# Relative-bias attention and squared-ReLU layers on one core: the turning of one batch's x by DMA, one ring of four PSUM banks, and a new order of the instructions

## The chip, the cores and the metric

The kernel runs on one core of a Trainium2 chip (trn2). The metric is the device time of one execution in microseconds; three runs of the kernel before are given, and the median counts. The profile comes from another execution of the same program, and its own span is the time against which sums are made. A core has five engines with a queue of instructions each: PE (TensorE, matmuls; its loads of the stationary operand are listed as PEld), DVE (VectorE), ACT (ScalarE), POOL (GpSimd) and SP (SyncE, which here only issues DMAs). Each engine works through its own queue in order and waits at an instruction until the semaphores that it names have come.

## The reference

Inputs are `q`, `k`, `v` of shape (8 batches, 8 heads, 576 positions, 64), a table of 32 buckets of bias by head, and two weight matrices, 512 x 2048 and 2048 x 512. What is computed, cut to its core:

```python
scores = scale * q @ k.T + bias_table[bucket(pos_i - pos_j)]
attn = exp(scores - max) / sum(exp(scores - max))
x = (attn @ v) -> 4608 tokens x 512
h = maximum(x @ w_in, 0)
out = (h * h) @ w_out
```

Beyond a distance of 128 all positions share one bucket, so the bias differs from a constant only in a band around the diagonal.

## The kernel before

**Tiles and stages.** A pair is two heads of one batch; there are 32 pairs, four to a batch. For a pair, q and k come from memory as 16-bit numbers into a stage buffer (`stg`, ring of 5), are turned so that the head's 64 numbers lie on partitions (`qt`, `kt`, ring of 4), and the scores are computed with keys on partitions: `run` (L698 to L725) makes four score matmuls of 512 columns (L707) into two PSUM sets (`st`, two banks each, ring of 2), and ACT takes the exponential from there into `pt` (L720). As 576 is 4.5 times 128, the last 64 queries and keys of a pair are done apart: corners of `qt` and `kt` are copied into the buffer `qz` (L689, on DVE or POOL), `last_queries` (L733) and `last_keys` (L758) make their scores, L743 and L768 their exponentials. DVE multiplies the band of `pt` with the table of exponentials of the bias (L801). P.V follows (L837, L844) in two parts of 3 and 2 tiles of 128 queries, each part in one PSUM bank, a column of ones giving the sums; DVE takes reciprocals (L861) and normalises into `x` (L866).

**Turning x.** The layers need x with its features on partitions (`xt`, a ring of three batches). `x_turn` (L894) does it on PE: four transposes of 128 x 128 for each of five tiles (L904), and an eviction by ACT or DVE (L624, L626). It serves the batches under `DT_X` (2). The batches from `DT_X` on are turned by two DMA transposes a pair, issued on SP (L879 to L892). Likewise q and k of batches 0 and 1 are turned on PE (L662), and those of later batches by DMA from SP (L645).

**Layers.** The 4608 tokens are nine groups of 512. In layer 1 (L1257) a group has 16 tiles of four matmuls of 512 columns; ACT applies the relu (L1286), DVE squares (L1296). Layer 2 (`second`, L991) uses Strassen's scheme with seven products instead of eight: sums of the weights (L958) and of the activations (L983) on DVE, then products of 16 matmuls of 256 columns (L1028), collected by fused adds on DVE (L1056) or copies on ACT (L1062). In the last two groups part of layer 1 is done by sevens too (`by_sevens`, L1116): a unit replaces 4 of the 16 tiles by seven products of four matmuls of 256 columns (L1182), with the sums of L1108 and the collecting operations L1207, L1212, L1221, L1230 and L1232. `UNITS` gives the number of units, one for group 7 and two for group 8.

**PSUM.** Eight banks: four for the score sets, one for P.V (`pv_ps`, ring of 1), three for everything else (`g_ps`: table, transposes, layers 1 and 2, ring of 3).

**What sets the order.** Every operation is first put into a plan with its engine or engines, its supposed duration, its dependences, its buffers, a due time and an earliest time (`Plan.add`, L105). `Plan.schedule` (L113) then walks through a model of the engines: at each step it takes, of the operations that can start first, the one that is due first, and gives it a buffer of its ring. The instructions are issued in that order, so the plan's durations and due times decide the order in every queue, and what a wait is placed behind. `LAT` holds supposed delays between engines, `SWITCH` the price of a change between kinds of matmul on PE (modes "c", transposes of 96 rows; "r", scores; "f", all else). `load` puts a DMA's issue on POOL or SP and its transfer on a modelled DMA engine.

**Loads.** POOL issues the loads that cast (q, k, weights, v of batches 0 and 1; L280); v of later batches comes as 32-bit numbers by SP and is cast by POOL (L556). Small fills (L398, with the constants `QUIET` and `LATER` as earliest times) prepare buffers; `s_fix` (L415) are the ten fills of the stages.

```python
def xt_free(upto):
    old = upto - 1 - XR
    return [f1_last[old // GT]] if old >= 0 else []
```

`f1_last` holds the operation of layer 1 that was added last for a group, and a write into `xt` waits for it.

Of the kernel before, what the change touches and what calls it, by code (L numbers as in the profile page):

```python
# [33 lines left out]
DT_X = 2  # L34
RELU_DVE = 0
NSTG, NQK, NPT, NV, NX, NGB, NRT, NY, NF = 5, 4, 3, 3, 6, 2, 4, 4, 2
QUIET, LATER = 5000.0, 9000
# [6 lines left out]
UNITS = {7: 1, 8: 2}  # L44
# [7 lines left out]
def _bucket(n):  # L52
    half = NBK // 2
    max_distance = 128
    log_ratio = np.log(np.maximum(n, 1).astype(np.float32) / half) / np.log(
        max_distance / half
    )
    large = half + (log_ratio * (half - 1)).astype(np.int32)
    large = np.minimum(large, NBK - 1)
    return np.where(n < half, n, large).astype(np.int64)  # L60

# [36 lines left out]
SWITCH = 105.0  # L98


class Plan:
# [11 lines left out]
    def schedule(self):  # L113
# [12 lines left out]
        while len(done) < len(self.ops):  # L126
            best = None
            for e in engines:
                pick = None
                for op in waiting[e]:  # L130
                    at = max(now[e], op.ready, self._buf_time(op))
                    if at == float("inf"):
                        continue
                    key = (max(at, now[e]), op.due if op.due > -1e8 else op.ready - 1e9, op.seq)
                    if pick is None or key < pick[0]:
                        pick = (key, op)
                if pick is None:
                    continue
                if best is None or pick[0][0] < best[0][0]:
                    best = (pick[0], e, pick[1])  # L140
            assert best is not None, "the plan is stuck"
            (at, _, _), e, op = best
            took = op.engs[e]
            if e == "PE" and op.mode != mode:
                took += SWITCH
                mode = op.mode
            for x in op.engs:
                waiting[x].remove(op)
            op.eng, op.start, op.end = e, at, at + took
            now[e] = op.end  # L150
            for b in op.bufs:
                if b.slot is None:
                    t, b.slot = min(b.ring.free)
                    b.ring.free.remove((t, b.slot))
                    b.ring.taken += 1
                b.left -= 1
                b.until = max(b.until, op.end + LAT[e])
                if not b.left:
                    b.ring.free.append((b.until, b.slot))
            for u in op.users:  # L160
                u.wait -= 1
                if not u.wait:
                    u.ready = max(
                        [u.after]
                        + [d.end + (LAT[d.eng] if tuple(u.engs) != (d.eng,) else 0.0) for d in u.deps]
                    )
                    for x in u.engs:
                        waiting[x].append(u)
            done.append(op)
# [15 lines left out]
def mm(n):  # L185
    return n / 2.4 + 2.5
# [11 lines left out]
def kernel(  # L198
# [64 lines left out]
    pv_ps = [psum.tile([128, 512], FP32, name=f"pv{i}") for i in range(1)]  # L263
    g_ps = [psum.tile([128, 512], FP32, name=f"f{i}") for i in range(3)]

    P = Plan()
    r_set, r_pv, r_g, r_lane = Ring(2), Ring(1), Ring(3), Ring(8)
# [7 lines left out]
    def loader(eng_name, eng, out_, in_, packets, deps=(), bufs=(), due=0.0, after=0.0, turn=-1e9):  # L275
# [3 lines left out]
            {eng_name: 720.0 if eng_name == "POOL" else 600.0},  # L279
# [77 lines left out]
    for c in range(6):  # L357
# [11 lines left out]
        o = P.add({"PE": 16 * 55.0}, t_mm, [o_eb, l_oh], [t_b], LEAD + TAB, 0.0, "f")  # L369
# [27 lines left out]
    def fill(ap, value, ns, due, after, deps=()):  # L397
        return P.add({"DVE": ns}, lambda: io(nc.vector.memset(ap, value)), deps, (), due, after)  # L398

    zz = z_sb.bitcast(FP32)  # L400
# [15 lines left out]
        fill(stg[i][w][96:128, 512:640].bitcast(FP32), 0.0, 90.0, 40 + i, 25000.0)  # L416
# [25 lines left out]
    def load_six(p, w):  # L442
# [8 lines left out]
                192 * 75, (), [b_stg[p]], pdue(),  # L451
# [3 lines left out]
    def load_rows(p, w):  # L455
# [8 lines left out]
                512 * 34.5, s_fix, [b_stg[p]], pdue(),  # L464
            )
            for e in range(2)
# [5 lines left out]
                128 * 34.5, s_fix, [b_stg[p]], pdue(),  # L472
# [14 lines left out]
    def load_v_head(b, h):  # L487
# [4 lines left out]
            512 * 34.5, v_fix[min(b, 1)], [b_v[b]], pdue(),  # L492
# [3 lines left out]
    def load_v_tail(b):  # L496
        for e in range(2):
# [4 lines left out]
                256 * 34.5, v_fix[min(b, 1)], [b_v[b]], pdue(),  # L502
# [4 lines left out]
    def load_v(b):  # L507
        for tt in range(4):
# [4 lines left out]
                1024 * 34.5, v_fix[min(b, 1)], [b_v[b]], pdue(),  # L513
# [7 lines left out]
    def load_v_fp32(b):  # L521
# [9 lines left out]
        for tt in range(5):  # L531
            fb = Buf(r_f)
            if tt < 4:
# [5 lines left out]
                        1024 * 19, 760.0,  # L539
                    )  # L540
                ]
            else:
# [5 lines left out]
                        256 * 19, 420.0,  # L548
# [15 lines left out]
    def load_w_in(u):  # L564
# [5 lines left out]
                512 * 102, (), (), pdue(),  # L570
# [3 lines left out]
    def load_w_out(u):  # L574
# [4 lines left out]
            512 * 102, (), (), pdue(),  # L579
# [54 lines left out]
    def pair(p):  # L634
# [5 lines left out]
        for w, dst in ((0, qts), (1, kts)):  # L640
            if b >= DT_QK:
# [9 lines left out]
                evac.append(P.add({"DMA": 1160.0}, None, [o], [qb, b_stg[p]], -1e9))  # L651
# [19 lines left out]
            o = P.add({"PE": 12 * 36.0 if b < SIX else 5 * mm(128)}, tr, l_qk[p, w] + [l_id], [bank, b_stg[p]], T - 3000, after, "c" if b < SIX else "f")  # L671
# [11 lines left out]
        for w, src, dst in ((0, qts, qzs), (1, kts, kzs)):  # L683
            for e in range(2):
# [6 lines left out]
                spread.append(one_of({"DVE": 200.0, "POOL": 320.0} if b < DT_QK else {"POOL": 320.0}, sp, [evac[w]] + z_fix[min(p, 1)], [qb], T - 1000))  # L691
# [135 lines left out]
        for part, qt0, nq in ((0, 0, 3), (1, 3, 2)):  # L827
# [49 lines left out]
            if b >= DT_X:  # L877
# [10 lines left out]
                t = x_last[hp, part] = P.add({"DMA": 232.0 * nq}, None, [t], [xb], -1e9)  # L888
# [35 lines left out]
    def xt_free(upto):  # L924

        old = upto - 1 - XR
        return [f1_last[old // GT]] if old >= 0 else []
# [188 lines left out]
    def by_sevens(g, units, due):  # L1116
# [22 lines left out]
        for u in range(units):  # L1139
# [30 lines left out]
            for n, i in enumerate((1, 6, 2, 5, 7, 3, 4)):  # L1170
# [17 lines left out]
                o = f1_last[g] = P.add(  # L1188
# [3 lines left out]
                )  # L1192
                to, plus, where = reads[i]
# [44 lines left out]
    def layers(g):  # L1238
# [35 lines left out]
        for i in range(16):  # L1274
            if i >= skip and g < NG:
# [5 lines left out]
                f1_last[g] = o  # L1281
# [44 lines left out]

    for op in P.schedule():
# [32 lines left out]
```

The softmax here doesn't subtract the row's maximum and nothing guards it: scores larger than these inputs give would overflow.

## Time and profile before

| what | value |
|---|---|
| runs | 371.63 us (median), 371.18 to 372.67 |
| profiled execution, first to last instruction | 369.4 us |
| instructions | 10030 |
| DMA packets, bytes | 162293, 44.26 MB |
| DMA issues on POOL, of q and of k | 55.4 us x79 and 55.3 us x79 |
| x turned on PE (L904) | 40 matmuls, 3.4 us |
| x turned by DMA (L882) | 48 issues, 1.19 us each (median) |
| layer 1 (L1257), layer 2 (L1028, largest group) | 127.8 us x656, 36.1 us x288 |
| by sevens, collecting adds (L1207) | 15 of 0.69 us |

The page gives the span of the profiled execution and not the time around it; the median of the runs is 2.2 us above that span. Where the page or an answer names a line, that is the line of the kernel before. "A <- B" among the waits means that the engine of A stood idle until B was done; times there are the total, the count and the longest. Durations of matmuls overlap their neighbours, so two starts are a better price than one duration. The row "DMA to landing" of a tile counts from the start of the issue to the semaphore that tells of the transfer's end.

### The profile page before, as it was taken

The numbers are of one execution on the slowest core, as the hardware profiler recorded it, in microseconds if no ns is written. First come the engines' busy times: TensorE is split into PE (matmuls) and PEld (weight loads), VectorE is DVE, ScalarE is ACT, GpSimd is POOL, SyncE is SP. The second block draws the span as 40 slices with busy tenths as digits, with TensorE's granted clock in tenths as the row PEclk, the third lists the DMA queues.
The fourth block names the chain that finished last, engine by engine and source line by source line (L and its number), as shares of the span: only waits on it lengthen the run. The fifth ranks groups of instructions, "written<-read, shape, count | busy, mean of one in ns | idle before, by whom it ended". The sixth has DMA issues, their size and how long they took to land.

```text
span 369.4 us, 10030 instructions
## 1 busy us (share of the span) xinstructions
PE 353.9 (96%) x3966; PEld 246.0 (67%) x3966; DVE 277.0 (75%) x618; ACT 262.5 (71%) x377; POOL 185.4 (50%) x343
## 2 busy tenths in 40 slices
PE   3978999899999999999999999999999999999996
PEld 2656455556587457877785468745876689657885
DVE  3997789957785498658965687669755987888693
ACT  4998989688575887689766887688758880586420
POOL 8897359295655676757845556777614100000000
PEclk9999999999999999999999999999999999999999
DMA  9999999795999999998999999999985112200022
GB/s 171 156 135 172 187 175 93 96 112 94 175 113 146 165 128 140 132 167 150 125 130 149 114 161 108 157 169 141 108 124 130 46 36 63 88 2 28 30 86 87
DMA packets 162293, 44.26 MB, mean 120 GB/s; under 512 B 145734, under 2 KB 162246, under 8 KB 162246
## 3 DMA queue, kind: packets, MB, share of 16 engines
q0 software_dynamic: 74208, 14.53, 52.0%
q1 hardware_dynamic: 87696, 28.80, 42.2%
q8 instruction: 31, 0.51, 0.6%
q10 hardware_dynamic: 342, 0.30, 0.3%
q14 instruction: 16, 0.13, 0.1%
HBM read 36.88 MB, written 9.44 MB: 125 GB/s over the span
## 4 chain that ended last, share of the span: by engine, by line
PE 88%; DVE 7%; ACT 2%; DMA 1%; issue 1%; ACTq 0%; DVEq 0%
PE f L1257 32%; PE f L1028 29%; PE pv L844 9%; PE st L707 8%; PE pv L837 2%; DVE pt L801 2%; PE st L758 2%; PE st L733 2%; PE st L1182 1%; DVE x L866 1%; DMA g<-in_q_dram 1%; PE f L662 1%; PE f L363 1%; ACT pm L768 1%; PE pv L1182 1%; DVE s L983 1%
## 5 line engine op out<-in xcount | busy, mean ns | idle before, releaser
L720 ACT ACTIVATE pt<-st 128x1024 f16<-128x1024 f32 x128 | 127.4, 1026 | 30.8 <-PE st L707 30.8
L1257 PE MATMUL f<-xt,w_in_sb 128*128 128x512 f16 (+4 forms) x656 | 127.8, 338 | 0.2 <-ACT xt L624 0.2
L1286 ACT ACTIVATE rt<-f 128x512 f16<-128x512 f32 x132 | 77.8, 602 | 38.4 <-PE f L1257 35.3
L1257 PEld LDWEIGHTS <-w_in_sb 128*128 128x128 f16 x656 | 57.9, 98 | 52.1 <-issue 12.2
L1296 DVE TENSOR_TENSOR g<-rt 128x512 f16<-128x512 f16 x132 | 57.6, 441 | 20.8 <-ACT rt L1286 19.8
L801 DVE TENSOR_TENSOR pt<-pt,tb_sb 128x1536 f16<-128x1536 f16 (+2 forms) x96 | 60.7, 640 | 15.6 <-ACT pt L720 15.1
L1028 PEld LDWEIGHTS <-g 128*128 128x128 f16 x576 | 54.5, 98 | 13.0 <-issue 4.7
L280 POOL DMA_DIRECT2D qs<-in_q_dram x79 | 55.4, 716 | 4.4 <-DMA w_out_sb<-in_moe_w_out_dram 2.6
L280 POOL DMA_DIRECT2D ks<-in_k_dram x79 | 55.3, 702 | 0.7 <-issue 0.6
L844 PE MATMUL pv<-va,pt 128*128 128x65 f16 x1280 | 54.7, 193 | 0.0
L844 PEld LDWEIGHTS <-pt 128*128 128x128 f16 x1280 | 50.2, 97 | 3.2 <-issue 1.4
L1056 DVE SCALAR_TENSOR_TENSOR y<-f,y 128x512 f32<-128x512 f32 (+1 forms) x47 | 31.4, 667 | 23.8 <-PE f L1028 23.6
L1028 PEld LDWEIGHTS <-s 128*128 128x128 f16 x432 | 41.2, 98 | 9.0 <-issue 2.5
L707 PE MATMUL st<-qt,kt 64*128 64x512 f16 x256 | 40.3, 385 | 0.9 <-ACT pt L743 0.4
L689 POOL COPY qz<-kt 64x64 f16<-64x64 f16 x58 | 18.5, 319 | 44.4 <-DMA kt<-ks 34.7
L689 POOL COPY qz<-qt 64x64 f16<-64x64 f16 x61 | 18.9, 310 | 35.4 <-DMA qt<-qs 27.3
L837 PE MATMUL pv<-vm,pm 128*128 128x130 f16 x160 | 35.3, 221 | 1.2 <-DVE x L866 1.0
L1028 PE MATMUL f<-w_out_sb,s 128*128 128x256 f16 x288 | 36.1, 273 | 0.0
L1028 PE MATMUL f<-wt,g 128*128 128x256 f16 x288 | 35.7, 273 | 0.0
L1028 PE MATMUL f<-w_out_sb,g 128*128 128x256 f16 x272 | 34.5, 273 | 0.7 <-ACT y L1062 0.7
L866 DVE TENSOR_TENSOR x<-pv,r 128x384 f16<-128x384 f32 x64 | 31.4, 490 | 2.0
L983 DVE TENSOR_TENSOR s<-g,s 128x1024 f16<-128x1024 f16 x36 | 25.6, 711 | 0.4
(90 smaller groups left out, 338.7 us busy)
## 6 DMA issues: line engine op xcount, KB each, us to landing
out_dram<-y SPq DMA_DIRECT2D x34, 256.0 KB, 2.4
f<-in_v_dram SPq DMA_DIRECT2D x24, 256.0 KB, 4.3
qs<-in_q_dram POOLq DMA_DIRECT2D x48, 64.0 KB, 4.4
ks<-in_k_dram POOLq DMA_DIRECT2D x48, 64.0 KB, 3.5
w_in_sb<-in_moe_w_in_dram POOLq DMA_DIRECT2D x4, 512.0 KB, 7.2
w_out_sb<-in_moe_w_out_dram POOLq DMA_DIRECT2D x4, 512.0 KB, 10.6
qs<-in_q_dram POOLq DMA_DIRECT2D x7, 144.0 KB, 4.6
ks<-in_k_dram POOLq DMA_DIRECT2D x7, 144.0 KB, 5.5
```

The lines of the kernel that those rows point to most:

```text
L280: lambda: io(eng.dma_start(out=out_(), in_=in_())),
L689: io(eng.tensor_copy(out=dst[qb.slot][rw, rw], in_=src[qb.slot][rw, 512:576]))
L707: nc.tensor.matmul(sets_ps[st.slot][:, e, :], kt[rw, ts(jt, 128)], qt[rw, 0:512], start=True, stop=True,)
L720: nc.scalar.activation(out=p5(pts[pb.slot])[:, jt, :, 0:512], in_=sets_ps[st.slot], func=EXPF, scale=SCALE)
L801: io(nc.vector.tensor_tensor(out=a, in0=a, in1=t, op=MULT))
L837: nc.tensor.matmul(ps[:, i, :, :], pm[:, c : c + 128], vm[:, hp, :, 0:65], start=True, stop=False)
L844: nc.tensor.matmul(ps[:, i, e, :], pt[:, (2 * jt + e) * S + c : (2 * jt + e) * S + c + 128], va[:, jt, 2 * hp + e, 0:65], start=False, sto ...
L866: nc.vector.tensor_tensor(out=xs[xb.slot][:, qt0 : qt0 + nq, :].rearrange("p t (e d) -> p t e d", e=2), in0=ps[:, :, :, 0:64], in1=rs[rb.s ...
L1028: nc.tensor.matmul(home[bf.slot][:, ts(s_, HALF)], left(c, s_), right(c), start=(c == 0 and (s_ == 0 or apart) and (own or i not in before ...
L1257: nc.tensor.matmul(g_ps[bank.slot][:, a:z], w_in_sb[:, kk, ts(nt, 128)], xt_sb[:, kk, c : c + z - a], start=(kk == 0), stop=(kk == 3),)
L1286: io(nc.scalar.activation(out=rts[rb.slot], in_=g_ps[bank.slot], func=RELUF))
L1296: nc.vector.tensor_tensor(out=gs[gb1.slot][:, nt, :], in0=rts[rb.slot], in1=rts[rb.slot], op=MULT)
```

## The change

1. `DT_X` goes from 2 to 1: x of batch 1 is turned by DMA transposes on SP as that of the later batches. PE loses 20 transposes, ACT and DVE five evictions, SP gets eight transposes.
2. `pv_ps` and `g_ps` become one list of four banks with one ring: P.V takes any of them, as do layers 1 and 2 and the transposes.
3. `UNITS` gives group 7 two units: 12 tiles of layer 1 become 8, and 28 matmuls of 256 columns are added.
4. The plan's durations are altered (issues, packets, transposes, copies), an engine's next operation may start before the one ahead has ended (`OVER`), and dependences within an engine get a delay (`AGAIN`). `QUIET` and `LATER` are 1000, so the fills may come at the start. The ten fills of `s_fix` may go to POOL or DVE.
5. A table `DUES` replaces the due time of 135 operations by number, after the plan is made.
6. `f1_last` becomes a list: a write into `xt` waits for all operations of layer 1 of the older group.

```diff
-DT_X = 2
+DT_X = 1
-QUIET, LATER = 5000.0, 9000
+QUIET, LATER = 1000.0, 1000.0
-UNITS = {7: 1, 8: 2}
+UNITS = {7: 2, 8: 2}
+DUES = """
+24:58480 30:161030 31:56140 56:-23560 57:13220 58:-12190 60:-19700 61:14570 62:-30210 63:122610 64:-31640
...
+"""
+STAY = 0.0
+OVER = {"ACT": 123.0, "DVE": 85.0, "POOL": 40.0}
+AGAIN = {"ACT": 30.0, "DVE": 30.0}
...
-            now[e] = op.end
+            now[e] = op.end - (OVER.get(e, 0.0) if op.fn is not None else 0.0)
...
-    pv_ps = [psum.tile([128, 512], FP32, name=f"pv{i}") for i in range(1)]
-    g_ps = [psum.tile([128, 512], FP32, name=f"f{i}") for i in range(3)]
+    g_ps = pv_ps = [psum.tile([128, 512], FP32, name=f"f{i}") for i in range(4)]
-    r_set, r_pv, r_g, r_lane = Ring(2), Ring(1), Ring(3), Ring(8)
+    r_set, r_g, r_lane = Ring(2), Ring(4), Ring(8)
+    r_pv = r_g
...
+    def fill_late(ap, ns, due, after):
+        def emit(o):
+            io((nc.vector if o.eng == "DVE" else nc.gpsimd).memset(ap, 0.0))
+
+        o = one_of({"DVE": ns, "POOL": ns}, emit, (), (), due)
+        o.after = o.ready = after
+        return o
...
-        fill(stg[i][w][96:128, 512:640].bitcast(FP32), 0.0, 90.0, 40 + i, 25000.0)
+        fill_late(stg[i][w][96:128, 512:640].bitcast(FP32), 110.0, 1e5, 30000.0)
...
-                512 * 34.5, s_fix, [b_stg[p]], pdue(),
+                512 * 13.5, s_fix, [b_stg[p]], pdue(),
...
-                t = x_last[hp, part] = P.add({"DMA": 232.0 * nq}, None, [t], [xb], -1e9)
+                t = x_last[hp, part] = P.add({"DMA": 190.0 * nq}, None, [t], [xb], -1e9)
...
-        return [f1_last[old // GT]] if old >= 0 else []
+        return f1_last[old // GT] if old >= 0 else []
...
-                f1_last[g] = o
+                f1_last.setdefault(g, []).append(o)
...
+    for x in DUES.split():
+        i, due = x.split(":")
+        P.ops[int(i)].due = float(due)
     for op in P.schedule():
```

In the order in which the built program's instructions stand, the change shows so: PE begins layer 1 after all P.V matmuls of batch 0, as before, but with all 192 transposes of q and k done (168 before); the two parts of a pair's P.V mostly stand together; between first and last P.V of batch 1 stand other stretches of layers 1 and 2; the last P.V of the kernel stands after 100 of 128 tiles of layer 1 (before 112 of 132) and 36.5 of 63 products of layer 2 (before 47). DVE gets 22 corner copies (before 9), eight evictions of kt (before 6), POOL 106 corner copies (before 119). ACT makes 128 plain relus (before 132), 12 for the sevens (9) and 14 squares there (9).

## The prediction

> **What bounds the kernel now.** First the page: busy time, granted clock, chain.
>
> ```profile
> span 369.4 us, 10030 instructions
> ...
> PE 353.9 (96%) x3966; PEld 246.0 (67%) x3966; DVE 277.0 (75%) x618; ACT 262.5 (71%) x377; POOL 185.4 (50%) x343
> ...
> PEclk9999999999999999999999999999999999999999
> ...
> PE 88%; DVE 7%; ACT 2%; DMA 1%; issue 1%; ACTq 0%; DVEq 0%
> ```
>
> PE works 96% of the span at full clock, and the chain runs on it for 88%. The average hides two stages, so next the stretches of 10 us (columns: busy PE, PEld, DVE, ACT, POOL with instruction counts, clock, DMA share, GB/s).
>
> ```profile
> 0.00:10.00 10.00, 4.10 (x64) 2.89 (x65) 3.99 (x17) 4.73 (x7) 8.10 (x18) 1.00 0.95 173
> 10.00:20.00 10.00, 9.09 (x210) 6.79 (x207) 9.41 (x24) 9.99 (x15) 9.22 (x17) 1.00 1.57 153
> 20.00:30.00 10.00, 8.40 (x173) 5.92 (x173) 9.37 (x34) 9.20 (x13) 8.66 (x18) 1.00 1.42 126
> 30.00:40.00 10.00, 7.88 (x114) 5.10 (x111) 6.49 (x18) 8.86 (x13) 7.67 (x16) 1.00 1.20 190
> ...
> 60.00:70.00 10.00, 8.85 (x125) 6.56 (x122) 9.54 (x23) 6.76 (x10) 5.71 (x10) 1.00 0.79 72
> 70.00:80.00 10.00, 9.44 (x83) 5.48 (x81) 7.14 (x19) 8.81 (x15) 7.21 (x15) 1.00 1.03 112
> ...
> 200.00:210.00 10.00, 10.00 (x62) 5.09 (x61) 5.88 (x13) 9.13 (x14) 6.53 (x13) 1.00 1.04 130
> ```
>
> Up to 40 us DVE and ACT are full and PE waits for them; from 80 us on PE is full. So time can be won by taking work off PE, or from PE's holes before 80 us. The waits of PE say how little of the holes one cause holds (total, times, longest):
>
> ```profile
> PE f L662 <- ACT qs L481: 5.9, 1, 5.9
> PE f L904 <- DVE x L866: 1.3, 3, 0.6
> PE st L758 <- ACT pt L720: 1.3, 2, 0.8
> PE pv L837 <- DVE x L866: 1.0, 3, 0.5
> PE f L1028 <- ACT y L1062: 0.7, 1, 0.7
> ```
>
> Last the timeline of PE, for prices: start to next start, since durations overlap.
>
> ```profile
> 82.08 1.04 PE L1028 MATMUL f<-w_out_sb,s 128*128 128x256 f16 x8
> 82.96 0.39 PE L733 MATMUL st<-qz,kt 128*128 128x128 f16 x4
> 83.18 1.03 PE L1257 MATMUL f<-xt,w_in_sb 128*128 128x512 f16 x4
> 84.04 1.04 PE L1028 MATMUL f<-w_out_sb,s 128*128 128x256 f16 x8
> 85.01 0.60 PE L707 MATMUL st<-qt,kt 64*128 64x512 f16 x4
> 85.55 1.04 PE L1257 MATMUL f<-xt,w_in_sb 128*128 128x512 f16 x4
> ```
>
> A tile of layer 1 costs 0.865 us, eight matmuls of 256 columns 0.872 (0.109 each), last queries 0.23. Entering the scores adds 0.10 (85.01 against 84.04 + 0.87), leaving them 0.11; as these and the 96-row transposes run on other tile sizes, I count 0.105 per switch.
>
> **PE's bill before.** 132 tiles of layer 1 x 0.865 = 114.2; layer 2, 1008 x 0.109 = 109.9; by sevens, 84 x 0.109 = 9.2; 160 query tiles of P.V x 0.299 = 47.8; 64 score runs x 0.427 = 27.3; last queries and keys, 32 x (0.23 + 0.24) = 15.0; q and k transposes, 192 x 0.032 = 6.1; table and far 3.1; 40 transposes of x x 0.057 = 2.3; 149 switches x 0.105 = 15.6. Sum 350.5. The rest of 369.4 is 18.9: start 5.9; holes before the first tile of layer 1 (38.8, when 26.6 of the bill is done) 6.3; from 63 to 75 us 2.4; later 1.0; after the last matmuls 3.3. Medians of the runs (371.63) stand 2.2 above the span; I carry that over.
>
> **The change, by its parts.**
>
> *PE's work.* Batch 1's x leaves PE: 20 x 0.057 = -1.1. The second unit of group 7: -4 x 0.865 + 28 x 0.109 = -0.4. The built order has 152 switches: +0.3. Bill after: 349.3, so -1.2. These lie on the path wherever PE is full.
>
> *Sevens, other engines.* ACT gets 6 more operations net, x 0.54 = +3.2; DVE five fused adds x 0.63 less about five squares x 0.37 = +1.3. From 290 us to the end ACT shows 4 to 9 busy of 10 and DVE 7 to 9, so I price it at nothing; bare, it would be 1.3 to 3.2. The sums of weights were formed for group 8 anyway.
>
> *x of batch 1 by DMA.* Five evictions go (2.2 us of ACT and DVE at 70 us); eight transposes enter SP's queue at 1.19 each. What is late next is the landing, below.
>
> *One ring of four banks.* It can take away the 1.0 that P.V waits for the normalisation; below nothing it can cost as much, since layer 2's four banks now stand in P.V's way. I take 0 to -1.0, inside the holes.
>
> *Order: the start.* Until the first tile of layer 1 the end is set by DVE's last normalisation of batch 0 (37.83; first tile 0.98 later). In the new order DVE does before that: 13 more corner copies (L689), two more evictions x 0.67, three sums of weights x 0.40; less: fills worth 1.75 that move into DVE's idle wait for k (4.1 long), and ten fills of stages, 0.8, now on POOL. The copies cost 0.173 (the three of q) to 0.281 (the six of k), so 2.2 to 3.7: net +2.2 to +3.7. Against it DVE has 2.8 of holes there, 1.1 of them ended by ACT, which before its first relu gets two exponentials and two evictions less (-3.0). So the last normalisation falls between 37.2 (all holes gone, cheap copies) and 41.5 (none gone, dear copies); I take 38.5, nearest to the cheap copies, because POOL, their neighbour, has 9 of them less. First tile 39.5. PE then has 349.3 - 27.4 = 321.9 to do (before 323.9).
>
> [...]
>
> *Order: 60 to 80 us.* DVE again: from the tiles of x to the read of group 0's first product it has 25.2 us of work in its order (16 squares and 13 sums of weights among it), while PE has 24.9 (bill 27.4 to 52.3) in the same time. So PE still waits there, at least 0.3 and, with some holes in DVE, up to the 2.4 of before plus 0.6; I take 1.6. The two waits for x's transposes (1.3) have gone, the products' one remains.
>
> *The new wait.* PE's first tile of group 1 now waits for a DMA, and everything on PE is queued behind it. By the bill it comes 10.0 us after batch 1's last P.V. That ends at 39.5 + 29.3 + 1.6 = 70.4; normalised 71.3. On SP, in order, the last pair's first part is followed by a load of v (0.45) and three transposes; the last starts at about 70.4 + 1.19 + 0.45 + 2 x 1.19 = 74.4. Landing, by the row of x:
>
> ```profile
> DMA to landing us min/median/max: 2.3/3.7/6.4
> ```
>
> gives 76.7, 78.1 or 80.8 against a need at 80.4: hidden, with 2.3 to spare at the median, 0.4 short at the worst.
>
> [...] Here PE's row is 57 ns a block, and the landing lies under 10 us of other PE work.
>
> *The rest.* From 80 us on the new order moves attention ahead of layers 1 and 2: the last P.V comes at 267 of PE's bill, before at 296. Per batch that leaves PE 30 to 37 us, ACT 24 to 30, DVE 17 to 30, POOL 25 (24 loads x 0.65, 16 copies x 0.31, six casts): none is over PE. I keep the 1.0.
>
> **Sum.** 39.5 + 321.9 + 1.6 + 1.0 + 3.3 = 367.3, that is -2.1; on the median **369.5**.
>
> **Rivals.**
>
> 1. *Forecast* (0.44): as above, 368.5 to 370.5, three quarters of it beyond half a per cent.
> 2. *The start gives it back* (0.26): DVE takes the added copies and sums without losing its holes. First tile at 41.0, then 2.0: 41.0 + 321.9 + 2.0 + 1.0 + 3.3 = 369.2, so 371.4. For it: DVE is full from 10 to 30 us and gets work. Against: ACT has 3 us less. This is also the case that the change doesn't do what it says: P.V's wait goes, and its 1.0 was never the limit.
> 3. *The start gains* (0.14): last normalisation 37.2, then 0.8: 38.2 + 321.9 + 0.8 + 1.0 + 3.3 = 365.2, so 367.4.
> 4. *Slower: transfers come late* (0.16). One mechanism: SP and POOL issue in order, and the attention of batches 1 to 7 now wants its transfers about 12% faster (24 pairs in some 195 us, before 220). If a transpose of x sits behind one that waits for its stage, group 1's first tile stalls, PE with it. Each foreign transpose in front costs 1.2, a wait for a stage 3 to 6. It decides from 4 us of stall on (2.1 gained, 1.9 to be seen); at 6 us the time is 369.5 + 6 - 0.5 = 375.0. Against it: SP's 24 us and POOL's 25 per batch fit in 30.
>
> **Numbers.** Half a per cent, 1.9 us, is about what a measurement of this kernel can tell from no change. Faster: 0.33 + 0.01 + 0.14 = 0.48; same 0.11 + 0.22 + 0.03 = 0.36; slower 0.03 + 0.13 = 0.16. The range takes in case 3 and most of case 4: 367.0 to 374.5.
>
> **What would show it.** Right: 20 transposes of x and 28 more matmuls of 256 columns; first tile of layer 1 at 38.5 to 40.5; PE's holes from there to 80 us under 2.5; full from 80 us on; last P.V about 30 us earlier. Wrong: a PE wait for a DMA at group 1 or later (case 4), the first tile after 41 (case 2), a hole after 290 us (sevens).

## The result and the profile after

The changed kernel takes **400.21 us** (median of four runs, 398.86 to 400.35) where the kernel before took 371.81 beside it: a ratio of 1.075 (95% interval 1.072 to 1.078). The forecast of 369.5 and its whole range are missed, on the other side. The profiled execution has a span of 397.0 us, 27.6 more than before.

The page of the changed kernel (its lines are those of the kernel before plus some 30):

```profile
span 397.0 us, 10045 instructions
...
PE 362.5 (91%) x3958; PEld 251.4 (63%) x3958; DVE 277.4 (70%) x621; ACT 260.6 (66%) x378; POOL 184.8 (47%) x340
...
PEclk9977599998998999999999998999999999999999
...
PE 70%; DMA 15%; POOL 7%; DVE 4%; issue 2%; ACT 1%; SPq 0%; POOLq 0%; ACTq 0%
```

Three things differ. PE's idle time (span less busy) is 34.5 us and not 15.5: 19.0 more. PE's busy time is 8.6 longer, although its bill is 1.2 shorter: by this account 9.8 us are the same work done slower, and the row of the granted clock, all nines before (0.96 in the mean, before 1.00), says why. And the chain that ended last now runs for 15% over DMAs (before 1%) and for 7% over POOL. PE's waits name them (total, times, longest; left out is the wait at the kernel's start, 6.4 for a first load; before it was 5.9, for ACT's cast of the first q):

```profile
PE f L695 <- DMA qs<-in_q_dram: 7.5, 1, 7.5
...
PE st L791 <- POOL qz L722: 4.6, 3, 2.4
PE f L1291 <- DMA xt<-x: 3.5, 3, 2.1
PE f L695 <- DMA ks<-in_k_dram: 3.2, 1, 3.2
PE st L766 <- POOL qz L722: 2.8, 1, 2.8
```

None of these stood among the waits of before. The stretches (columns as in the prediction) give the places:

```profile
10.00:20.00 10.00, 8.91 (x202) 6.29 (x201) 9.55 (x22) 9.58 (x14) 10.00 (x15) 1.00 1.44 155
20.00:30.00 10.00, 5.59 (x71) 4.18 (x70) 8.05 (x24) 5.22 (x7) 7.49 (x14) 0.70 1.49 184
30.00:40.00 10.00, 7.10 (x114) 5.21 (x112) 6.70 (x16) 5.66 (x6) 5.08 (x10) 0.79 1.22 197
40.00:50.00 10.00, 5.45 (x77) 4.26 (x78) 1.81 (x6) 3.09 (x5) 3.33 (x14) 0.55 1.26 188
...
60.00:70.00 10.00, 10.00 (x93) 4.99 (x92) 9.96 (x29) 9.06 (x16) 3.11 (x3) 1.00 0.16 33
70.00:80.00 10.00, 9.82 (x139) 6.73 (x138) 9.82 (x22) 9.10 (x12) 8.38 (x12) 1.00 1.25 101
...
90.00:100.00 10.00, 7.57 (x47) 4.36 (x45) 4.23 (x7) 4.35 (x7) 8.71 (x19) 0.83 1.23 173
```

From 20 to 50 us not only PE but DVE and ACT are half empty, while the DMA column is as full as ever: everybody waits for loads. From 60 to 80 us all is well. At 90 us the next hole comes, again with a lower clock.

To place the loss I take, for a matmul, the time at which PE starts it less the bill of all matmuls ahead of it, which I call its **lag**. Before, it is 12.1 us at the first tile of layer 1 (38.8 us) and 15.5 at the end. After, it is 25.8 at the first tile (53.2 us), 26.1 at 86 us, 44.2 at 264 us, and stays there (to 0.1) to the end. So **13.7 us are lost before layer 1, and 18.5 after its first tile, nearly all between 86 and 264 us (before 3.4)**; the tail and the sevens lose nothing.

**The start.** PE's timeline (start, duration, in brackets the wait ahead):

```profile
36.69 0.41 PE L877 MATMUL f<-va,pt 128*128 128x65 f16 x8
44.55 0.69 PE L695 MATMUL f<-id_sb,qs 96*64 96x96 f16 x12 [7.46 <-DMA qs<-in_q_dram]
...
53.20 1.04 PE L1291 MATMUL f<-xt,w_in_sb 128*128 128x512 f16 x4
```

and POOL's, which issues the load that PE waits for:

```profile
24.33 0.77 POOL L305 DMA_DIRECT2D w_in_sb<-in_moe_w_in_dram  x1
25.09 1.51 POOL L305 DMA_DIRECT2D w_out_sb<-in_moe_w_out_dram  x2
...
26.82 0.74 POOL L305 DMA_DIRECT2D w_out_sb<-in_moe_w_out_dram  x1
...
28.57 1.39 POOL L305 DMA_DIRECT2D qs<-in_q_dram  x2 [0.41 <-DMA w_out_sb<-in_moe_w_out_dram]
```

Four loads of weights, 512 KB each, stand ahead of the last two loads of q of batch 1. In the trace they land at 33.4, 36.7, 40.1 and 43.4 us, and only then the two of q, at 44.5 and 45.4. Before, the last q or k of batch 1 landed at 36.5, and PE did not need it before layer 1. Now PE's order wants all 192 transposes first.

Two entries of the table put them there: `98:1400` and `94:5170` make the two issues due after the weights, which have their old due times (31 to 38). The plan saw no harm in it, since in its model a transfer goes by a due time of its own (`99:-22910` for one, an untouched 20 for the other) and may overtake the weights' transfers (34 to 38): by the plan's arithmetic, no measurement, they have landed by 30 us. In the traces of before and after the loads on POOL's queue land in the order of their issue, all 182 of each.

**Later.** The hole at 93 us, first POOL, then PE:

```profile
93.97 0.77 POOL L305 DMA_DIRECT2D ks<-in_k_dram  x1
94.78 0.51 POOL L722 COPY qz<-qt 64x64 f16<-64x64 f16 x2
```
```profile
95.52 0.54 PE L791 MATMUL st<-qt,qz 128*128 128x288 f16 x2 [2.43 <-POOL qz L722]
```

A corner copy stands behind loads of later pairs, which POOL issues without a break. At 242 us (1.7) it is much the same: loads, casts and other copies stand ahead. At 119 us (2.8 and 0.5) it is not: POOL itself stood still until the transposed q had landed, and only then could it copy. POOL, then PE:

```profile
118.78 0.98 POOL L722 COPY qz<-qt 64x64 f16<-64x64 f16 x4 [2.33 <-DMA qt<-qs]
```
```profile
119.24 0.38 PE L766 MATMUL st<-qz,kt 128*128 128x128 f16 x4 [2.82 <-POOL qz L722]
```

Two more, 0.8 at 137 and 2.1 at 186, are for transposes of x.

**The clock.** In stretches of 3.41 us, counted from where the clock record changes (busy PE first, the clock third from the end):

```profile
17.18:20.59 3.41, 1.98 (x24) 0.94 (x22) 3.26 (x9) 2.99 (x5) 3.41 (x6) 1.00 1.39 147
20.59:24.00 3.41, 3.41 (x49) 3.06 (x47) 3.35 (x13) 2.20 (x3) 1.51 (x3) 0.50 1.89 156
24.00:27.41 3.41, 1.03 (x11) 0.41 (x8) 3.35 (x9) 2.43 (x3) 3.36 (x6) 1.00 1.32 196
27.41:30.83 3.42, 1.75 (x26) 1.12 (x26) 0.77 (x3) 0.47 (x1) 2.02 (x6) 0.50 1.27 204
...
41.07:44.48 3.41, 0.00 (x0) 0.00 (x0) 0.00 (x0) 0.00 (x0) 0.00 (x0) 0.50 1.30 190
44.48:47.89 3.41, 3.34 (x44) 2.24 (x45) 0.49 (x2) 2.15 (x4) 1.77 (x10) 0.50 1.26 205
47.89:51.31 3.42, 3.42 (x51) 2.94 (x49) 2.33 (x9) 0.93 (x2) 2.87 (x7) 0.50 1.13 120
51.31:54.72 3.41, 3.34 (x35) 2.05 (x32) 2.27 (x7) 3.15 (x6) 3.41 (x6) 1.00 1.21 77
```

Behind the stretches with 1.98, 1.03 and, from 37.65 us, 0.00 us of busy PE the next one runs at a clock of 0.50, so PE does its work of 44.5 to 51.3 us, when the loads are there at last, at half clock. Nine stretches at half clock, 30.7 us, hold 24.6 us of busy PE. The kernel before has none after the start; its emptiest stretch is

```profile
21.29:24.70 3.41, 2.42 (x47) 1.64 (x41) 3.25 (x15) 3.41 (x5) 2.92 (x8) 1.00 1.81 159
```

### The profile page after: what moved, and what is told of

Its sections match the earlier page's. It is cut to its first block, busy times and chain, and to the rows that moved or that the text cites. A ratio compares the mean times of both kernels' runs of the same rounds, so it can differ in the third digit from the quotient of the medians.

```text
span 397.0 us, 10045 instructions
## 1 busy us (share of the span) xinstructions
PE 362.5 (91%) x3958; PEld 251.4 (63%) x3958; DVE 277.4 (70%) x621; ACT 260.6 (66%) x378; POOL 184.8 (47%) x340
## 3 DMA queue, kind: packets, MB, share of 16 engines
q1 hardware_dynamic: 90512, 29.45, 39.6%
## 4 chain that ended last, share of the span: by engine, by line
PE 70%; DMA 15%; POOL 7%; DVE 4%; issue 2%; ACT 1%; SPq 0%; POOLq 0%; ACTq 0%
PE f L1291 26%; PE f L1061 23%; PE f L877 7%; PE st L740 6%; DMA qs<-in_q_dram 4%; DMA qt<-qs 3%; DMA xt<-x 3%; DMA w_out_sb<-in_moe_w_out_dram 2%; POOL va L305 2%; PE st L791 2%; PE f L870 2%; POOL ks L305 2%; POOL qs L305 2%; PE st L1215 2%; PE f L1215 1%
## 5 line engine op out<-in xcount | busy, mean ns | idle before, releaser
L753 ACT ACTIVATE pt<-st 128x1024 f16<-128x1024 f32 x128 | 124.6, 1030 | 32.0 <-PE st L740 31.9
L1291 PE MATMUL f<-xt,w_in_sb 128*128 128x512 f16 (+4 forms) x640 | 130.4, 343 | 3.6 <-DMA xt<-x 3.5
L1320 ACT ACTIVATE rt<-f 128x512 f16<-128x512 f32 x128 | 75.5, 609 | 39.8 <-PE f L1291 32.9
L1291 PEld LDWEIGHTS <-w_in_sb 128*128 128x128 f16 x640 | 58.1, 99 | 51.4 <-issue 16.6
L1330 DVE TENSOR_TENSOR g<-rt 128x512 f16<-128x512 f16 x128 | 57.1, 452 | 42.1 <-ACT rt L1320 41.3
L834 DVE TENSOR_TENSOR pt<-pt,tb_sb 128x512 f16<-128x512 f16 (+2 forms) x96 | 59.4, 632 | 13.8 <-ACT pt L753 13.3
L877 PE MATMUL f<-va,pt 128*128 128x65 f16 x1280 | 55.0, 198 | 0.0
L877 PEld LDWEIGHTS <-pt 128*128 128x128 f16 x1280 | 52.6, 101 | 1.0
L1089 DVE SCALAR_TENSOR_TENSOR y<-f,y 128x512 f32<-128x512 f32 (+1 forms) x48 | 32.0, 666 | 15.5 <-PE f L1061 15.4
L870 PE MATMUL f<-vm,pm 128*128 128x130 f16 x160 | 36.5, 228 | 0.0
L722 POOL COPY qz<-qt 64x64 f16<-64x64 f16 x54 | 16.1, 301 | 43.3 <-DMA qt<-qs 11.8
L801 ACT ACTIVATE pm<-st 128x576 f16<-128x576 f32 x32 | 21.2, 664 | 17.0 <-PE st L791 16.7
L899 DVE TENSOR_TENSOR x<-f,r 128x384 f16<-128x384 f32 (+1 forms) x64 | 31.0, 487 | 1.1
```

The source lines that it names most:

```text
L722: io(eng.tensor_copy(out=dst[qb.slot][rw, rw], in_=src[qb.slot][rw, 512:576]))
L753: nc.scalar.activation(out=p5(pts[pb.slot])[:, jt, :, 0:512], in_=sets_ps[st.slot], func=EXPF, scale=SCALE)
L834: io(nc.vector.tensor_tensor(out=a, in0=a, in1=t, op=MULT))
L870: nc.tensor.matmul(ps[:, i, :, :], pm[:, c : c + 128], vm[:, hp, :, 0:65], start=True, stop=False)
L877: nc.tensor.matmul(ps[:, i, e, :], pt[:, (2 * jt + e) * S + c : (2 * jt + e) * S + c + 128], va[:, jt, 2 * hp + e, 0:65], start=False, sto ...
L1089: nc.vector.scalar_tensor_tensor(out=dst, in0=ps, scalar=OSC, in1=ys[y[plus].slot][:, cs], op0=MULT, op1=mybir.AluOpType.add,)
```

## The experiments

The first theories were these. **A**: the table of due times costs, by the order of the loads. **B**: the structural parts (x by DMA, shared banks, units) cost with any order. **C**: the new durations in the plan cost. Ratios are to runs of the kernel before on the same chip; "lag" is at the first tile of layer 1 and its growth from there to the end; "half" is the time at half clock between the start and the last matmul.

| run | us | ratio (95%) | first tile | lag, growth | half |
|---|---|---|---|---|---|
| before | 372 | | 38.8 | 12.1 + 3.4 | 0 |
| changed | 400.2 | 1.075 (1.072 to 1.078) | 53.2 | 25.8 + 18.5 | 30.7 |
| e1_no_table | 385.1 | 1.035 (1.031 to 1.039) | 42.9 | 16.1 + 14.7 | 13.7 |
| e2_weights_later | 405.8 | 1.088 (1.083 to 1.092) | 41.3 | 13.9 + 38.0 | 20.5 |
| e3_struct | 382.5 | 1.028 (1.022 to 1.034) | 40.0 | 14.2 + 17.8 | 10.2 |
| e4_consts | 382.8 | 1.029 (1.026 to 1.032) | 45.6 | 17.3 + 8.6 | 10.2 |
| e5_same_order | 391.9 | 1.052 (1.048 to 1.057) | 46.2 | 18.8 + 16.6 | 20.5 |
| e18_four_later | 391.2 | 1.052 (1.048 to 1.055) | 42.1 | 14.6 + 20.3 | 20.5 |
| e9_copies_ahead | 396.4 | 1.066 (1.062 to 1.069) | 47.9 | | 17.1 |
| e6_fill | 404.1 | 1.086 (1.081 to 1.091) | 60.1 | | 23.9 |
| e10_fill_right | 398.8 | 1.070 (1.064 to 1.077) | 54.3 | | 20.5 |
| e14_fill_long | 397.0 | 1.070 (1.063 to 1.076) | 52.3 | | 13.7 |
| e7_redraw_switch | 373.6 | 1.003 (1.001 to 1.005) | 40.0 | 13.4 + 4.9 | 3.4 |
| e11_quiet | 373.1 | 1.001 (0.999 to 1.003) | 39.7 | 13.0 + 4.1 | 0 |
| e12_turn | 375.5 | 1.009 (1.006 to 1.011) | 40.7 | 14.0 + 7.9 | 3.4 |
| e13_ring | 380.1 | 1.022 (1.016 to 1.028) | 39.6 | 13.8 + 11.4 | 6.8 |
| e15_dma | 384.5 | 1.032 (1.029 to 1.035) | 44.0 | 17.0 + 10.2 | 3.4 |
| e16_over | 376.6 | 1.012 (1.009 to 1.014) | 40.2 | 13.3 + 8.4 | 0 |
| e17_units | 373.4 | 1.003 (1.002 to 1.004) | 38.8 | 12.2 + 5.6 | 0 |
| e19_no_table_no_ring | 386.1 | 1.038 (1.033 to 1.043) | 43.8 | 15.5 + 17.0 | 17.1 |

No version beats the kernel before.

**The four first cuts.** e1 empties `DUES`; e2 keeps the full table and adds `116:5200 122:5210 124:5220 126:5230 130:5240`; e3 is the kernel before with `DT_X = 1`, the ring of four, `UNITS = {7: 2, 8: 2}` and the list `f1_last`; e4 is the kernel before with the new durations, fills, `OVER` and `AGAIN` (and the list `f1_last`).

> The changed kernel with its table of due times emptied: every other part (turning of x by DMA, ring of four, sevens, new durations in the plan) stays. The loads of q and k of batch 1 then stand ahead of all weights but one on POOL again. Theory A (the table is what costs, because the plan it was fitted to lets late loads overtake the weights in front of them): first tile of layer 1 back at 38 to 41 us, no wait of PE of more than 2 us for a load of q or k, clock at 1.00 after the start, time 368 to 373. Theory B (the turning of batch 1's x by DMA and the shared banks cost, with any order): the waits from 90 us on remain, 385 or more. Theory C (the new durations make the plan too tight): also 385 or more.

> The changed kernel with five due times added to its table, so that five loads of weights are issued behind the last two loads of q of batch 1 and not ahead of them. Theory A: these two land before 31 us, not at 44.5 and 45.4; PE's waits of 3.2 and 7.5 us for them go, with the half clock after them; the first tile of layer 1 comes at 39 to 42 and not at 53.2; the time falls by 11 to 14, to 386 to 390, since the later stalls have other causes. Theories B and C: the wait moves to something else in the start, first tile after 48, time over 394.

> The kernel before with the structural parts alone: batch 1's x turned by DMA, one ring of four banks, two units of group 7, the list of last operations; the plan's durations, fill times and due times stay those of before. Theory A: 368 to 374, with the first tile of layer 1 at 37 to 40. Theory B: 380 or more, with waits of PE for the turning of x. Theory C (durations): as A.

> The kernel before with the new durations, fill times and the fills of the stages that may go to POOL, and none of the structural parts nor the table. Theory A: 368 to 374. Theory B: as A. Theory C: 385 or more, with waits of PE for loads in the start and for corner copies on POOL later.

None of the three theories is enough. The table costs 15.1 us (400.2 to 385.1), 10.3 of it before the first tile: A is right for the start. But the rest without it still costs 12 to 13, the structural parts alone 10 and the new durations alone 10 to 11, so what B and C name costs as well (B's "with any order" is another matter, see e19), and the three do not add up. In e2 the two loads of q land at 28.7 and 29.4 and the first tile comes at 41.3, as A said; the time grows all the same, because the five due times made the plan draw a new order for all that follows (the plan's own span rises from 360.5 to 378.3 us), and that lag grows by 38 us. A plan cannot be changed in one place only, so the next cuts move instructions after the plan is made.

**The order kept, loads moved.** e5 moves five loads of weights (plan numbers below) behind load 94 in the finished order; e18 leaves 116, the first load of w_out, in its place; e9 adds to e5 that each corner copy on POOL goes ahead of up to eight loads before it.

```diff
-    for op in P.schedule():
+    row = P.schedule()
+    moved = [o for o in row if o.seq in (116, 122, 124, 126, 130)]
+    row = [o for o in row if o not in moved]
+    at = [o.seq for o in row].index(94) + 1
+    row[at:at] = moved
+    for op in row:
```

> The changed kernel with its whole order kept, except that on POOL's queue five loads of weights are moved behind the load of q that stood after them; PE, DVE, ACT and SP have the same instructions in the same order. Theory A (in the start PE stands for q and k that are queued behind weights): first tile of layer 1 at 40 to 43 us (53.2 in the changed kernel), and as nothing later is touched its later stalls of 18.5 stay: about 12 less, 386 to 391, a wait of up to 3.5 us for a weight included. Rival (the start is held by something else, DVE or POOL's copies): first tile after 48, time over 395.

> The changed kernel with its order kept, and on POOL's queue four loads of weights moved behind the late loads of q instead of five: the first load of w_out, which DVE's first sum of weights waits for, stays where it was. Theory A with that wait as the rest: the wait of PE of 2.6 us behind DVE goes, with some of the half clock; first tile of layer 1 at 42 to 44.5 (46.2 with five moved), time 2 to 4 under the 391.9 of that run, 387 to 390. Rival (the rest of the start is DVE's and ACT's own work): first tile at 46, 391 to 393.

> As the run with five loads of weights moved behind, and further on POOL's queue alone: each corner copy is moved ahead of up to eight loads that stood directly before it, as far as its own transpose allows. Theory E (after the start PE loses its time to corner copies that stand behind loads on POOL's queue): PE's waits for POOL, 7.4 us in the changed kernel, fall under 3, a stretch or two of half clock goes too, and the time is 5 to 10 below that of the run without this move. Rival (the loads moved back are then late themselves, so the wait only changes its name to the transposes of q and k): within 3 of it, with longer waits for qt, kt or xt.

e5 gains 8.3 us with nothing changed but the place of five DMA issues on one queue, and the first tile comes 7.0 earlier. That it stayed at 46.2 has a cause that the waits of DVE and PE's timeline show:

```profile
DVE wt L991 <- DMA w_out_sb<-in_moe_w_out_dram: 2.9, 1, 2.9
```
```profile
40.07 0.62 PE L877 MATMUL f<-va,pt 128*128 128x65 f16 x8 [2.64 <-DVE pt L834]
```

A sum of weights on DVE wants the first of the moved loads, and DVE holds up PE. With that load left in place (e18) the first tile comes at 42.1, as expected. So the start is settled: of the 14.4 us by which the first tile was late, 11.1 go by moving four issues. The time, though, is 391.2 and not 387 to 390, 9.0 less than the changed kernel: the later lag grows by 20.3 in place of 16.6, 1.5 of it a new wait for w_in. e9 refutes theory E. Its waits for POOL are longer, not shorter (9.0 in all, 7.8 in e5), and the one for DVE has doubled (2.6 in e5; lines after 722 are one higher here):

```profile
PE st L767 <- POOL qz L722: 7.1, 2, 4.9
...
PE f L878 <- DVE pt L835: 5.6, 1, 5.6
```

A copy that is moved ahead waits for its own transpose and holds the loads behind it: POOL stands still for 2.76 us until a transposed q lands at 109 us, and the wait of 4.9 comes at 116. It was 4.2 in e5, where POOL had also stood still for a late transposed q (1.95 us), as at 119 us in the changed kernel. Sorting copies against loads does not bring a transpose earlier.

**The clock by itself.** Useless matmuls keep PE at work while it waits; the transposes then overwrite their bank. e6 put them at the wrong pairs, e10 at the right ones, e14 has 62 for 42.

```diff
+FILL = {(6, 1): 17, (4, 0): 62}
             def tr(w=w, bank=bank):
...
+                for _ in range(FILL.get((p, w), 0)):
+                    io(nc.tensor.matmul(g_ps[bank.slot][:, 0:384], id_sb, tb_sb[:, 0, :], start=True, stop=True))
```

> The changed kernel with 17 and 42 useless matmuls of 384 columns on PE, ahead of the two groups of transposes that wait 3.2 and 7.5 us for k and q, into the bank that the transposes then overwrite; all else is the same. The waits end when the loads land, so the work itself gains nothing. Theory A1 (the half clock after a stretch with little work on PE is a price of its own, on top of the wait): the clock stays at 1.00 from 24 to 51 us, where the changed kernel ran 5.2 + 6.8 us of work at half; first tile of layer 1 at 49 to 51, time 2.5 to 5 less, 395 to 398. Theory A2 (the half clock is hidden, since ACT and DVE set the pace there): first tile at 53, 400; or more, as the added work delays.

> As the run with useless matmuls, but ahead of the two groups of transposes that really stood still (17 before a k of the third pair of batch 1, 42 before the last q of batch 1's start); in the run before they stood one group off and PE did them after its waits. Theory A1 (the half clock is a price of its own): clock 1.00 from 27 to 51 us, first tile of layer 1 at 48.5 to 51.5 (53.2 in the changed kernel), time 395.5 to 398.5. Theory A2 (half clock hidden behind ACT and DVE): first tile at 53, 400.

> As the run with useless matmuls ahead of the right transposes, with 62 in place of 42 ahead of the last q, since those 42 ended 3.1 us before the load landed and the clock still went to half from 45.8 to 52.6 us. The load lands at 44.5 to 45.6 as before. Theory A1 (the half clock is a price of its own): clock 1.00 from 27 us to the first tile of layer 1, which comes at 49 to 51, and 395 to 397. Theory A2 (ACT and DVE set the pace from the load to the first tile, the half clock is hidden): first tile at 53 to 54, 399 to 401.

e6 decides nothing on the clock: PE waited first and did the useless work afterwards, 8.7 us of it, partly at half clock (the same 42 took 7.0 in e10), and the time rose by 3.9. In e10 the matmuls ended 3.1 us before the load came; one stretch with 0.34 us of work, and the clock was at half from 45.8 to 52.6 again. In e14 they last:

```profile
36.22 10.24 PE L692 MATMUL f<-tb_sb,id_sb 128*128 128x384 f16 x62
46.39 0.45 PE L697 MATMUL f<-id_sb,qs 96*64 96x96 f16 x12
...
52.30 1.90 PE L1293 MATMUL f<-xt,w_in_sb 128*128 128x512 f16 x8
```

Twelve transposes take 0.45 us there, in the changed kernel at half clock 0.69, and from the first late transpose to layer 1 it takes 5.9 us and not 8.65 (44.55 to 53.20), for the same matmuls and with no wait of PE in either. So the half clock costs **2.7 us here, beyond the wait**: A1. The first tile gains less, since the useless work ends later than the load had landed. Whether 13 us of work that nobody needs make the whole kernel faster is not shown: the medians are 3.2 us apart (397.0 against 400.2), but its runs lie between 396.6 and 401.8, and the intervals of the two ratios overlap.

**The parts, one at a time, on the kernel before.** Is any new order simply a worse one? e7 counts a change of mode 110 and not 105 in the plan, which redraws most of PE's order. Then single parts: e11 `QUIET, LATER = 1000.0, 1000.0`; e12 `DT_X = 1`; e13 the ring of four; e15 the durations of DMA work; e16 `OVER` and `AGAIN`; e17 `UNITS = {7: 2, 8: 2}` with the list. e19 takes the ring of four out of e1.

> The kernel before with one supposed duration of its plan altered a little: a change of mode on PE counts 110 and not 105. Nothing that is computed or issued changes, only the order that the plan makes. Theory D (the order of the kernel before is a lucky or a chosen one, and any new order from such a plan loses some 10 us, which is what the structural parts alone and the new durations alone cost): 378 to 386, with waits of PE for corner copies on POOL and for ACT spread over 60 to 250 us. Theory A (the parts of the change have costs of their own): 370 to 375.

> The kernel before with one part of the new constants alone: the small fills may come from 1 us on, not 5 and 9. The loads of v, which wait for these fills, then go ahead of six loads of q and k on POOL's queue; PE's order stays as it was. Theory F (the start of every version with the new constants, first tile at 42.9 and 45.6, is late because v goes ahead of q and k): first tile at 42 to 46, time 375 to 380. Rival (the start of these versions is late for their order on PE, DVE and ACT): first tile at 38.5 to 40, time 371 to 373.

> The kernel before with batch 1's x turned by DMA and nothing else. Theory G (of the structural parts, this one costs the 10 us): 378 to 384, with waits of PE from 60 us on for xt, or for qt and kt whose transposes stand behind those of x on SP. Theory H (the ring of four costs it: P.V, layer 1 and layer 2 take each other's banks): 371 to 374 here.

> The kernel before with one ring of four banks and nothing else. Theory H: 378 to 384, with waits of PE for DVE and ACT in stretches where P.V and layer 2 share banks. Theory G: 370 to 373.

> The kernel before with the plan's new durations of DMA work alone (issue on SP, packets of q, k, v and the weights, transposes); fills, copies, overlap and delays within an engine stay. Theory I (shorter supposed transfers let the plan put loads and copies tighter on POOL and SP than the chip does them): 376 to 382, with half of the 10 us that all new durations and fills cost, in waits of PE for loads and for corner copies. Rival (the overlap within an engine is the cause): 371 to 374.

> The kernel before with the overlap and delay within an engine alone: the plan lets the next operation start 123 (ACT), 85 (DVE) and 40 ns (POOL) before the one ahead has ended. Theory J (with it the plan thinks ACT, DVE and POOL faster than they are, so their queues fall behind and PE waits for them): 376 to 382, first tile of layer 1 after 41 us. Rival (transfers are the cause): 371 to 374.

> The kernel before with two units of group 7 by sevens in place of one, and nothing else. By the bill of PE 0.4 less; ACT and DVE get 3.2 and 1.3 us more in the tail. Theory of the prediction (hidden there): 370.5 to 373. Rival (the added sums of weights and activations move what stands before 80 us, and PE waits): 374 to 377.

> The changed kernel without its table and with P.V in a bank of its own again (rings of one and three). Theory K (the costs of the parts add up): 385.1 less the 7.7 of the ring alone, 375 to 380. Rival (with the new durations the order is set by other things, and the ring costs nothing more): 382 to 387.

D falls: this new order costs 1.0 us (0.4 to 1.7), so not any new order loses ten. It is one order only; e12, e13 and e16 redraw PE's order too, and such an amount may be in their prices. F falls: the earlier fills cost nothing that can be told from the noise. Among the structural parts G and H share: the turning costs 3.2 (2.2 to 4.1), the ring 8.0 (5.8 to 10.3). The mechanisms that they named do not show: with x turned by DMA PE has no wait for `xt`, and more for DVE's normalisation (2.6, before 1.0) and for one `kt` (1.1); with the ring its longest waits after the start are for ACT's exponentials (2.0 and 1.8), and for a reader of a shared bank none is over 0.9. Of the ring's 8, PE's idle time is 4.7 (20.2 against 15.5) and its busy time grew by 4.5 with a smaller bill; two stretches are at half clock, each behind one with a hole, in which PE is busy for 1.79 and 1.85 us (the first, in stretches of 3.41 us of e13):

```profile
30.43:33.84 3.41, 1.79 (x14) 0.83 (x14) 3.00 (x9) 3.15 (x5) 1.70 (x5) 1.00 1.10 171
33.84:37.26 3.42, 3.20 (x46) 2.86 (x44) 1.48 (x6) 1.61 (x3) 3.07 (x6) 0.50 1.08 162
```

Of the durations, both cost: the transfers 12 (I, more than it said), the overlap 4.3 (J in its low end, though the first tile came at 40.2, not after 41). With shorter supposed transfers PE's waits (e15) are those of the changed kernel, in small:

```profile
PE f L662 <- DMA qs<-in_q_dram: 3.2, 1, 3.2
PE st L733 <- POOL qz L689: 2.6, 1, 2.6
```

The units cost 1.1 us (0.6 to 1.6), and the one new wait of PE in the tail (e17) is

```profile
PE f L1258 <- ACT rt L1287: 1.2, 1, 1.2
```

at 329 us. The lag of e17 is that of before up to 316 us and grows by 2.1 from there, so this cost is the sevens' and not a new order's. K falls: without the ring, e1 is not faster (386.1 against 385.1). With the new durations the ring costs nothing more that these runs can tell.

The plan's own arithmetic, its span before any measurement, tells two kinds of cost apart. With the old durations it is 375.8 us for the kernel before, where the chip needs 369.4, and it grows with the parts: by 1.6 for e7, 2.6 for e17, 4.6 for e12, 5.3 for e13 and 10.2 for e3, where the measured times grow by 1.0, 1.1, 3.2, 8.0 and 10. So the structural parts make a longer plan, and the plan's span said so beforehand; why they do is not shown. With all the new durations it is the other way: for the changed kernel the plan gives 360.5, 15 less than for the kernel before, and the chip needs 397.0; for e15 and e16 the plan moves by 2.2 and -0.8, the chip by 12 and 4.3. For e1, e4 and e19 the chip is 14 to 20 behind the plan, for e7, e12, e13, e17 and e3 it is 2 to 7 ahead. That the old durations, where they were too long, gave the in-order queues their slack fits all of these, but no run shows it by itself.

## Why the prediction was wrong, point by point

- **PE's bill** was right: 20 transposes of x, 28 more matmuls of 256 columns, and the lag is flat from 264 us to the end, with prices from the rows of before.
- **The start is the step that failed.** "Until the first tile of layer 1 the end is set by DVE's last normalisation of batch 0": this looked for what was late next on one engine only, and so put the waits of PE for loads of q and k at nothing. They are 10.7 us, and the half clock behind them comes on top. The view that showed it was at hand: the order of POOL's queue, with six loads of weights ahead of the last q, the last four landing 3.3 us apart, against a PE order with 192 transposes ahead of layer 1 and not 168. The shift of 24 transposes was known, and nobody asked when their loads would land. Predicted 39.5, measured 53.2; with four of those loads moved behind (e18) 42.1.
- **60 to 80 us**: 1.6 of holes forecast; the lag grows by 0.3 there. That is luck: the late start had given DVE 14 us more for its work. In e18, whose first tile comes at 42.1, the lag grows by 2.3 over the same stretch of PE's bill, within the 0.3 to 3.0 that were thought possible.
- **The new wait for x** was hidden at group 1, as worked out; its tile came at 95.85 after a wait for POOL, not for x. At groups further on transposes of x cost 0.8 and 2.1, which nobody asked about. Alone, the turning costs 3.2 us where the bill gave 1.1 less, though PE in that run (e12) has no wait for x's transposes.
- **"The rest. I keep the 1.0"** failed too: 18.2. Sums of work per batch (POOL 25 of 30 to 37 us) say that a queue can hold its work, not that each piece comes in time when loads and copies stand in one line.
- **The ring** at 0 to -1.0: alone +8.0. It was weighed by the one wait that it removes, not by the order that it makes.
- **The sevens** at nothing: right in the changed kernel, where no hole opens after 290 us; alone they cost 1.1 (0.6 to 1.6), about the lower end of the bare price of 1.3 to 3.2.
- **POOL beside DVE's copies**: no run shows that DVE's copies get cheaper when POOL has fewer, the reason given for 38.5. What the traces show: 22 copies on DVE after, median 0.178 us, one of 0.572; copies of this size beside a copy of POOL took 0.157 to 0.216, before and after. Beside the longest of before, 0.574 at 21.31 us, POOL did not copy but issued a load, and the copy ended within 0.02 us of the end of that issue; so did the long ones of after (0.572, 0.440 and 0.366).
- **Rival 4** had the right kind of mechanism (transfers late in queues that run in order) at chance 0.16, with one stall of 6 us for x at group 1; there were two long ones elsewhere, for q and k in the start, and a row of short ones.
- **The clock** was in no case at all. The row of before showed full speed throughout, and I took it as a constant. By PE's busy time it is worth 9.8 of the 27.6 us; at the one place where it was tested it cost 2.7. By estimate, half of its length, one stretch of 3.41 us at half clock costs 1.7 at most.

What stays open: how the 18.5 us after the first tile divide among the parts of the change. In the trace the waits for copies and transposes named above are 10.3 of them, and the three stretches at half clock from 90 us on at most 5 by the same estimate. The new durations and the structural parts each bring such a growth alone (8.6 and 17.8), but in no version did it go while the new order stayed, and moving copies on POOL did not help.

## What to carry to other kernels

Where an order is planned with supposed durations, look first at what the plan may believe and the chip does not do: here, that one load can overtake others on the same queue. For each engine that gets more to do ahead of a stage, list the loads that this work needs with their place in their queue and add up their landings; a sum per engine does not show it. And before pricing a hole on PE at its length, look at how much work stands around it: in the changed kernel, from 10 us on, each stretch of 3.41 us in which PE had 1.98 us of work or less was followed by one at half clock, and at the one place where that was tested it cost 2.7 us beyond the wait.

## What the hardware showed that was not expected

In the changed kernel the granted clock is 1.00 or 0.50 and changes at whole multiples of 3.41 us: at 20.59, 24.00, 27.41, 34.24, 41.07, 51.31, 95.68, 99.09, 119.57, 122.99, 242.45 and 245.87 us. Between the start of its clock record (10.35) and the last matmul (393.9), the stretches at full clock with 0.00, 0.59, 0.98, 1.03, 1.53 and 1.98 us of busy PE were followed by half clock. The emptiest of all others, 2.05 us from 184.43 on, was followed by full clock, and so was every stretch of the kernel before up to its last matmul, where the emptiest held 2.42; in e13 it was half clock after 1.79 and 1.85. From half clock the changed kernel went back after six stretches with 2.93 to 3.41, and not after those with 0.00 and 1.75, nor after one with 3.34. What decides it, these few stretches do not show.

Loads on POOL's queue landed in the order of issue (182 of 182, before and after), and a load of 144 KB behind four loads of 512 KB took 15.9 us from issue to landing (28.57 to 44.51), against a median of 5.7 for the seven of its kind in the first 70 us.
